# Moving the start of activation tiles by 0 to 64 bytes inside their slots, in a kernel of attention and two MoE layers

## The chip, the cores and the metric

The kernel runs on one core of a Trainium2 chip. The metric is the device time of one execution in microseconds. Before the change the median of three runs is 848.98 us (847.02 to 849.09).

## The reference

```python
# attention, per batch and head: softmax of q over the head dimension, of k over the sequence
q_s = exp(q - max(q, -1)); q_s /= sum(q_s, -1) + 1e-9
k_s = exp(k - max(k, 2));  k_s /= sum(k_s, 2) + 1e-9
kv = einsum('bhsd,bhse->bhde', k_s, v)
x = einsum('bhsd,bhde->bhse', q_s, kv)        # 4 batches, 8 heads, 576 rows, 64 columns
x = x.transpose(0, 2, 1, 3).reshape(2304, 512)
# first MoE: weights 512x2048 and 2048x512
h = x @ w_in
g = where(h >= 1, h, where(h <= -1, 0, (h + 1)**2 / 4))
x = g @ w_out
# second MoE, the same sizes
h = x @ w_in2
g = h * tanh(log1p(exp(h)))
out = g @ w_out2
```

Everything is float32.

## The kernel before

The 2304 tokens are worked in six blocks of 384 (`TB`, line 23). The first MoE and the second are done one after the other; attention for later blocks is fed in between the matmuls of earlier ones.

**Split operands.** From block 1 of the first MoE on, a float32 operand is kept as two tiles of type float32r, a high part (ScalarE copies and rounds the value) and a low part (VectorE or GpSimd subtracts the high part from the value). A product is then three matmuls: weights high by activation high, weights low by activation high, weights high by activation low (`three`, lines 510 to 513). Block 0 of the first MoE uses plain float32 matmuls instead (line 529), and so does the second layer there for its first 12 of 16 slices (line 590).

**First MoE, from block 1.** `gemm1` (line 523) makes one 128-column slice of the hidden layer in 12 matmuls of 128x384; the weights are the stationary operand, and the tiles `xh` and `xl` (made by `x_tiles`, line 262) are the moving one. The slice passes through ScalarE and VectorE, `split_high` (line 542) allocates a tile `ghl`, whose first half is the high and whose second half the low part, and three slices later (`LAG`, line 25) `gemm2` (line 582) reads it in 12 more matmuls (line 601), again as the moving operand.

**Second MoE.** It is worked in seven products instead of eight per 2x2 group of blocks (the sums that this needs are made beforehand). `unit` (line 710) makes the hidden layer: each of seven products is 6 matmuls of 128x384 with weights stationary and the activation tiles `xc` moving (allocated in `x_high`, line 703). The results are stored to DRAM and read back as `gq`, and `g_split` (line 766) splits each into two tiles `gc`. `product` (line 787) computes the output: 21 products of 72 matmuls of 128x256. Here the roles are turned round: 128-column pieces of `gc` are the stationary operand, loaded by a weight load (PEld), and the weight tiles `w2p` and `w2q` are the moving one (line 799).

**Where the tiles lie.** There are two large pools in SBUF. Weights and some activations are in pool `wp` (`big`): 36 slots of 4,096 bytes per partition. Everything else of this section is in pool `ap` (`small`, lines 119 and 120): 22 slots. A slot is as large as the largest tile of its tag. That is `v_t`, 96x2x6x65 float32 elements, 3,120 bytes a partition, which the layout rounds up to 3,136 bytes. An activation tile, 2x384 elements, takes the first 3,072 bytes of its slot. As 3,136 is 24.5 times 128, neighbouring slots begin at two places that alternate in a stretch of 128 bytes: odd slots 32 bytes and even slots 96 bytes into it. In a stretch of 256 bytes slots 0, 1, 2, 3 begin at 224, 32, 96 and 160, and then again. All weight tiles of pool `wp` begin 224 bytes into such a stretch, and so do all the pieces of them that a matmul reads, since these are 512 or 1,024 bytes apart.

**Order of the work.** The first block runs from a list of steps written out by hand (`STARTUP`). For the rest of the first MoE's blocks 1 to 4 the order on ScalarE and SyncE is the program's, that on the other engines a scheduler's (`REGIONS`, line 28); from block 5 on the order on all engines is the program's. Which slot a tile gets follows from the order in which slots come free.

Of the kernel before, what the change touches and what calls it, by code (L numbers as in the profile page):

```python
# [11 lines left out]
F32R = mybir.dt.float32r  # L12
# [7 lines left out]
P = 128  # L20
R = 96
J = 6
TB = 384
# [36 lines left out]
)  # L60
ROUND = 768.0


@with_exitstack
def tile_attention_two_moes(
# [17 lines left out]
    NP = H // 2  # L83
# [7 lines left out]
    ap = ctx.enter_context(tc.tile_pool(name="ap", bufs=22))  # L91
# [19 lines left out]
    def f(ap):  # L111
        return ap.bitcast(F32)
# [5 lines left out]

    def small(shape, dtype, name):
        return ap.tile(shape, dtype, tag="s", name=name)  # L120

    def bank(name):

        if ready:
            return a_p.tile([P, 512], F32, tag="a", name=name)
        return acc_p.tile([P, 512], F32, tag="acc", name=name)
# [16 lines left out]
    def w_stages(ph, c, m):  # L143
# [17 lines left out]
        def rounded():  # L161
            sg = f(st["t"])[:, :, 1]
            nc.scalar.activation(out=sg, in_=sg, func=AF.Copy, bias=ROUND)

# [37 lines left out]
        def sums():  # L202
            r = quarters[m, u].rearrange("p r c x -> p (r c) x")
            t = st["s"] = [small([P, 2, 2 * P], F32, "ws") for _ in range(2)]
            if m:
                t2, t3, t1, _ = (t[i // 2][:, i % 2] for i in range(4))
                add(nc.vector, t1, r[:, 1], r[:, 0])
                add(nc.gpsimd, t3, r[:, 3], r[:, 1])
                add(nc.vector, t2, r[:, 3], t1)
            else:  # L210
                s1, s2, s3, _ = (t[i // 2][:, i % 2] for i in range(4))
                add(nc.vector, s1, r[:, 2], r[:, 3], False)
                add(nc.gpsimd, s3, r[:, 0], r[:, 2])
                add(nc.vector, s2, s1, r[:, 0])
# [45 lines left out]
    xh, xl = {}, {}  # L260

    def x_tiles(ph, n):
        if n == 0:
            xh[ph, n] = [small([P, 2, TB], F32, "x0") for _ in range(NP // 2)]
            return
        xh[ph, n] = [small([P, 2, TB], F32R, "xh") for _ in range(NP // 2)]
        xl[ph, n] = [small([P, 2, TB], F32R, "xl") for _ in range(NP // 2)]

    def head_rows(a, b, c, j0, nj):
        return a[b, 2 * c:2 * c + 2].rearrange("h (p j) d -> p h j d", j=J)[:, :, j0:j0 + nj, :]  # L270
# [126 lines left out]
    def q_task(b, c, nc_, j0, nj, n, o):  # L397
# [86 lines left out]
        def x_high():  # L484
            ps = st["ps"] = st["x"][:, :nc_ * w].rearrange("p (c t) -> p c t", c=nc_)
            if (1, n) not in xh:
                x_tiles(1, n)
            st["at"] = (c // 2, (slice(None), slice(c % 2, c % 2 + nc_), slice(o, o + w)))
            i, at = st["at"]
            nc.scalar.activation(out=xh[1, n][i][at], in_=ps, func=AF.Copy)  # L490
# [5 lines left out]
        def x_split():  # L496
            x_high()
            x_low()

        if n < 2:  # L500
            return dict(
                L=load, max=row_max, sub=below, exp=exp, sum=row_sum, mul=over_sum, T=transposed, cp=copied,
                x=product, hi=x_high, lo=x_low,
            )
# [35 lines left out]
        return s[:2] == (1, 0) and s[2] < WHOLE  # L540

    def split_high(s):
        t = small([P, 2, TB], F32R, "ghl")
        gh[s], gl[s] = t[:, 0, :], t[:, 1, :]
        nc.scalar.activation(out=gh[s], in_=temps[s], func=AF.Copy)  # L545

# [3 lines left out]
    def split_g(s):  # L550
        if s[1]:
            split_high(s)
            split_low(s, eltwise(s))
# [88 lines left out]
    def high_part(hi, x):  # L642
        nc.scalar.activation(out=hi, in_=x, func=AF.Copy)  # L643

    def low_part(eng, lo, x, hi):
        eng.tensor_tensor(out=lo, in0=x, in1=f(hi), op=ALU.subtract)  # L646
# [29 lines left out]
    xq, xc = {}, {}  # L676
# [24 lines left out]
        nc.sync.dma_start(out=t, in_=src)  # L701

    def x_high(g, k, get):
        xc[g, k] = [get([P, 2, TB], F32R, "xc") for _ in range(2)]
        high_part(xc[g, k][0], xq[g, k])

    def x_low(g, k):
# [49 lines left out]
    gq, gc, sums = {}, {}, {}  # L757
# [7 lines left out]

    def g_split(at, i):
        if at < len(products):
            gc[at, i] = hi, lo = [small([P, 2, TB], F32R, "gc") for _ in range(2)]
            x = gq.pop((at, i))
            high_part(hi, x)  # L770
            low_part(nc.vector, lo, x, hi)
# [15 lines left out]
    def product(at, steps):  # L787
# [46 lines left out]
        for i in pairs:  # L834
            for which in range(2):
                for j in range(CH):
                    mm(i, j, which)
            for job in steps.pop((at, i), []):
                job()
            g_split(at + 1, i)  # L840
            g_load(at + 2, i)
# [75 lines left out]
    def startup():  # L917
        nc.vector.memset(half, 0.5)
        nc.vector.memset(unround, -ROUND)
        nc.scalar.activation(out=table, in_=half, func=AF.Exp)  # L920
# [15 lines left out]
        for c in range(NF):  # L936
            s = (1, 0, c)
            tasks[f"act{c}"] = dict(a=partial(act_scaled, s), c=partial(act_squared, s), g=partial(act_least, s), h=partial(split_high, s), l=partial(split_low, s, nc.vector))
# [77 lines left out]
    def x_operand(table, at, g, k, fetch, keep, apart):  # L1016
        put(table, at - (apart == 1), x_fetch, g, k, fetch)
        put(table, at + apart, x_high, g, k, keep)
        put(table, at + apart + 1, x_low, g, k)
# [16 lines left out]
    for g in groups[1:]:  # L1036
        for x, k_ in enumerate(ORDER):
            keep = (big if x < 3 else small) if g == 1 else big if 3 <= x < 6 else small
            at = g * per_group + (3 * x - 24 if x < 3 else 2 * x - 18)
            x_operand(places, at, g, k_, small if x in (3, 5) else big, keep, 6)  # L1040
    for u in units:
        at = groups[-1] * per_group + per_unit + u * 11 // 2
# [10 lines left out]
    for i in pairs:  # L1053
        put(places, end - 16 + i, g_load, 0, i)
        put(places, end - 8 + i, g_load, 1, i)
        put(places, end - 8 + i, g_split, 0, i)
# [3 lines left out]
    at = NF  # L1060
    for engines, upto in REGIONS:
# [3 lines left out]
        at = upto  # L1065
    with region(None):
        slot(len(slots) + LAG)
        for g in groups:
            for u in units:
                at = (g * len(units) + u) * per_unit  # L1070
# [40 lines left out]
```

## Time and profile before

| | |
|---|---|
| median of three runs | 848.98 us (847.02 to 849.09) |
| span of the profiled execution | 846.4 us |
| TensorE matmuls (PE), busy | 834.9 us, 99% of the span, 5218 instructions |
| weight loads (PEld), busy | 796.9 us, 94% |
| VectorE (DVE), busy | 582.9 us, 69% |
| ScalarE (ACT), busy | 485.9 us, 57% |
| GpSimd (POOL), busy | 350.6 us, 41% |
| 16 DMA engines, share of the span in hardware queue 1 | 63.4% |

The page gives the span of the profiled execution, from its first to its last instruction, and no other time of it; the median of the runs is 2.6 us above this span. Matmuls are pipelined, so the duration of one (some 340 ns for 384 columns) is longer than the distance from its start to the next one's start. A row of the chain that merges matmuls, such as "2.08 PE acc L601 x12", gives the time from the first one's start to the start of what follows, so 2.08 divided by 12 is the distance from start to start; a row of the timeline that merges x matmuls ends with the whole duration of the last one.

### The profile page before, as it was taken

To read this page: it belongs to the slowest core of one execution; us is meant where nothing else is said; L and a number is where in the kernel's file an instruction comes from. 1 tells how busy PE (TensorE), PEld (TensorE's weight loads), DVE (VectorE), ACT (ScalarE), POOL (GpSimd) and SP (SyncE) were. 2 spreads that over 40 slices of the span, in tenths; PEclk is the share of its full clock that TensorE was granted. 3 is DMA by queue.
4 is the path that set the end of the run, shared out by engine and by line. 5 is a ranking of instruction groups with operands and counts; after the bars stand their busy time and mean duration, and the time that the engine had idled before them with its cause. 6 is when DMAs were issued, how large, how long until landed. Compare 5 with 4: busy or idle time off the path is not lost.

```text
span 846.4 us, 14671 instructions
## 1 busy us (share of the span) xinstructions
PE 834.9 (99%) x5218; PEld 796.9 (94%) x5218; DVE 582.9 (69%) x967; ACT 485.9 (57%) x837; POOL 350.6 (41%) x325
## 2 busy tenths in 40 slices
PE   8899999999999999999999999999999999999998
PEld 8556689999999999999999999999999999999998
DVE  6999989787767676655448447765777859475553
ACT  3888687766766776676558444332444565453621
POOL 3101336424655564533455236586666566000000
PEclk9999999999999999999999999999999999999999
DMA  9999102245947462544597067877787897867933
GB/s 241 311 307 215 38 1 81 70 99 145 257 128 212 141 191 96 177 139 159 188 323 261 19 217 250 282 273 276 289 278 254 322 365 250 258 236 219 328 91 101
DMA packets 139993, 171.24 MB, mean 202 GB/s; under 512 B 57360, under 2 KB 109584, under 8 KB 139920
## 3 DMA queue, kind: packets, MB, share of 16 engines
q1 hardware_dynamic: 139680, 170.10, 63.4%
q8 instruction: 41, 0.67, 0.3%
q14 instruction: 32, 0.26, 0.1%
q10 hardware_dynamic: 240, 0.20, 0.1%
HBM read 108.40 MB, written 61.87 MB: 201 GB/s over the span
## 4 chain that ended last, share of the span: by engine, by line
PE 90%; DMA 3%; DVE 3%; SPq 2%; ACT 1%; issue 1%; POOL 0%; DVEq 0%; ACTq 0%; POOLq 0%
PE acc L601 21%; PE o L799 19%; PE m L512 7%; PE m L511 7%; PE m L513 7%; PE h L511 7%; PE h L513 7%; PE h L512 7%; PE h L529 3%; PE acc L590 2%; PE xps L482 2%; DMA gq<-gd 1%; PE kv L366 1%; DMA q_t<-in_q_dram 1%; PE qT L467 1%; SPq L308 1%
## 5 line engine op out<-in xcount | busy, mean ns | idle before, releaser
L601 PE MATMUL acc<-ghl,parts 128*128 128x384 f32 x1008 | 191.7, 339 | 0.0
L601 PEld LDWEIGHTS acc<-ghl,parts 128*128 128x128 f32 x1008 | 176.2, 188 | 0.8
L799 PE MATMUL o<-w2p,gc 128*128 128x256 f32 x1296 | 152.3, 280 | 0.6 <-POOL w2p L646 0.6
L799 PEld LDWEIGHTS o<-w2p,gc 128*128 128x128 f32 x1296 | 151.9, 189 | 0.8 <-POOL w2p L646 0.8
L643 ACT ACTIVATE gc<-gq 128x768 fp32r<-128x768 f32 x84 | 70.6, 846 | 76.5 <-DMA gq<-gd 53.4
L646 DVE TENSOR_TENSOR gc<-gq,gc 128x768 fp32r<-128x768 f32 x84 | 90.3, 1107 | 32.1 <-ACT gc L643 30.6
L511 PE MATMUL h<-xh,parts 128*128 128x384 f32 x320 | 112.0, 350 | 0.0
L567 DVE SCALAR_TENSOR_TENSOR rg<-h,rg 128x384 f32<-128x384 f32 x96 | 53.0, 552 | 81.9 <-ACT rg L562 79.8
L513 PE MATMUL h<-xh,parts 128*128 128x384 f32 x320 | 107.8, 337 | 0.0
L512 PE MATMUL h<-xl,parts 128*128 128x384 f32 x320 | 107.5, 336 | 0.0
L558 ACT ACTIVATE rg<-h,half 128x384 f32<-128x384 f32 x96 | 55.4, 577 | 82.8 <-PE h L513 73.8
L548 POOL TENSOR_TENSOR ghl<-rg,ghl 128x384 fp32r<-128x384 f32 x63 | 69.7, 1107 | 78.0 <-ACT ghl L545 74.9
L512 PE MATMUL m<-xc,w2p 128*128 128x384 f32 x288 | 96.9, 336 | 0.0
L511 PE MATMUL m<-xc,w2p 128*128 128x384 f32 x288 | 96.6, 335 | 0.0
L513 PE MATMUL m<-xc,w2p 128*128 128x384 f32 x288 | 96.6, 335 | 0.0
L736 ACT ACTIVATE high<-high 128x768 f32<-128x768 f32 x24 | 20.3, 847 | 96.9 <-DVE high L247 42.4
L512 PEld LDWEIGHTS h<-xl,parts 128*128 128x128 f32 x320 | 60.2, 188 | 1.5
L511 PEld LDWEIGHTS h<-xh,parts 128*128 128x128 f32 x320 | 60.1, 188 | 1.5
L513 PEld LDWEIGHTS h<-xh,parts 128*128 128x128 f32 x320 | 60.1, 188 | 0.0
L156 DVE SCALAR_TENSOR_TENSOR wraw<-wraw 128x512 uint32<-128x512 uint32 x64 | 57.2, 893 | 2.0
L247 POOL TENSOR_TENSOR s<-high 128x384 f32<-128x384 f32 x24 | 26.6, 1107 | 74.8 <-ACT high L736 71.7
L545 ACT ACTIVATE ghl<-rg 128x384 fp32r<-128x384 f32 x84 | 43.5, 518 | 19.3 <-DVE rg L567 17.6
(110 smaller groups left out, 1559.8 us busy)
## 6 DMA issues: line engine op xcount, KB each, us to landing
gq<-gd SPq DMA_DIRECT2D x84, 384.0 KB, 6.8
gd<-s SPq DMA_DIRECT2D x48, 384.0 KB, 3.3
wraw<-in_moe_w_in_dram SPq DMA_DIRECT2D x32, 512.0 KB, 5.9
wraw<-in_moe_w_out_dram SPq DMA_DIRECT2D x32, 512.0 KB, 4.7
gd<-low SPq DMA_DIRECT2D x24, 384.0 KB, 3.6
wk<-ws SPq DMA_DIRECT2D x32, 256.0 KB, 4.4
w<-wk SPq DMA_DIRECT2D x16, 384.0 KB, 4.3
v_t<-in_v_dram SPq DMA_DIRECT2D x32, 144.0 KB, 5.1
```

The costliest lines, as they stand in the source:

```text
L156: nc.vector.scalar_tensor_tensor(out=t[:, :, 0], in0=t[:, :, 1], scalar=3, in1=t[:, :, 0], op0=ALU.logical_shift_left, op1=ALU.bitwise_xor,)
L511: nc.tensor.matmul(ps, ah, bh, start=start, stop=False)
L512: nc.tensor.matmul(ps, ah, bl, start=False, stop=False)
L513: nc.tensor.matmul(ps, al, bh, start=False, stop=stop)
L545: nc.scalar.activation(out=gh[s], in_=temps[s], func=AF.Copy)
L548: eng.tensor_tensor(out=gl[s], in0=temps.pop(s), in1=f(gh[s]), op=ALU.subtract)
L558: nc.scalar.activation(out=t[:, 0, :], in_=hs[s][:, :TB], func=AF.Relu, scale=0.5, bias=half)
L567: nc.vector.scalar_tensor_tensor(out=g, in0=hs[s][:, :TB], scalar=1.0, in1=r, op0=ALU.max, op1=ALU.min)
L601: nc.tensor.matmul(acc[key][x][:, :TB], *pairs[at], start=first and at == 0, stop=last and at == 2)
L643: nc.scalar.activation(out=hi, in_=x, func=AF.Copy)
L646: eng.tensor_tensor(out=lo, in0=x, in1=f(hi), op=ALU.subtract)
L799: nc.tensor.matmul(ps[j][:, :QUARTER], a[:, c, js], b, start=i == c == which == 0 and b is wh, stop=i == pairs[-1] and c == which == 1,)
```

## The change

A tuple of 13 offsets (in elements of 4 bytes) is added, and a helper that allocates a flat tile of 784 elements and returns a view of 768 of them that begins 0, 4, 8, 12, 16, 6, 2, 14, 10, 1, 8, 4 or 12 elements into it. The offsets are taken in turn over all tiles that the helper makes. `xh`, `xl`, `ghl`, `gc` and those `xc` that lie in pool `ap` come from it; an `xc` in pool `wp`, the plain float32 tiles of block 0 and every other tile stay as they are. The new tile has 3,136 bytes a partition.

```diff
+SHIFTS = (0, 4, 8, 12, 16, 6, 2, 14, 10, 1, 8, 4, 12)
...
+    placed = []
+
+    def shifted(name):
+
+        at = SHIFTS[len(placed) % len(SHIFTS)]
+        placed.append(at)
+        t = ap.tile([P, 2 * TB + 16], F32R, tag="s", name=name)
+        return t[:, at:at + 2 * TB].rearrange("p (c t) -> p c t", c=2)
...
-        xh[ph, n] = [small([P, 2, TB], F32R, "xh") for _ in range(NP // 2)]
-        xl[ph, n] = [small([P, 2, TB], F32R, "xl") for _ in range(NP // 2)]
+        xh[ph, n] = [shifted("xh") for _ in range(NP // 2)]
+        xl[ph, n] = [shifted("xl") for _ in range(NP // 2)]
...
-        t = small([P, 2, TB], F32R, "ghl")
+        t = shifted("ghl")
...
-        xc[g, k] = [get([P, 2, TB], F32R, "xc") for _ in range(2)]
+        xc[g, k] = [shifted("xc") if get is small else get([P, 2, TB], F32R, "xc") for _ in range(2)]
...
-            gc[at, i] = hi, lo = [small([P, 2, TB], F32R, "gc") for _ in range(2)]
+            gc[at, i] = hi, lo = [shifted("gc") for _ in range(2)]
```

## Rows read from the trace of the kernel before

**Rows 1.** The page: span, busy time of TensorE, granted clock in 40 slices.
```profile
span 846.4 us, 14671 instructions
...
PE 834.9 (99%) x5218; PEld 796.9 (94%) x5218; DVE 582.9 (69%) x967; ACT 485.9 (57%) x837; POOL 350.6 (41%) x325
...
PEclk9999999999999999999999999999999999999999
```

**Rows 2.** The chain of work that ended last: shares of the span by engine.
```profile
PE 90%; DMA 3%; DVE 3%; SPq 2%; ACT 1%; issue 1%; POOL 0%; DVEq 0%; ACTq 0%; POOLq 0%
```

**Rows 3.** Waits of TensorE: the four longest; us in total, times, longest.
```profile
PE qT L467 <- POOL q_e L455: 3.0, 2, 1.7
PE h L529 <- DVE rg L567: 2.6, 3, 1.5
PE warm L946 <- POOL ident masks.py:199: 1.4, 1, 1.4
PE o L799 <- POOL w2p L646: 0.6, 1, 0.6
```

**Rows 4.** Groups of matmuls by line and form; count, then busy us, mean ns.
```profile
L601 PE MATMUL acc<-ghl,parts 128*128 128x384 f32 x1008 | 191.7, 339 | 0.0
L799 PE MATMUL o<-w2p,gc 128*128 128x256 f32 x1296 | 152.3, 280 | 0.6 <-POOL w2p L646 0.6
L511 PE MATMUL h<-xh,parts 128*128 128x384 f32 x320 | 112.0, 350 | 0.0
...
L511 PE MATMUL m<-xc,w2p 128*128 128x384 f32 x288 | 96.6, 335 | 0.0
...
L799 PE MATMUL o<-w2q,gc 128*128 128x256 f32 x216 | 25.7, 280 | 0.0
...
L511 PE MATMUL m<-xc,w2q 128*128 128x384 f32 x48 | 16.1, 334 | 0.0
```

**Rows 5.** The chain, 413 to 482 us: start us, us, what; one `ghl` tile each.
```profile
456.20 2.08 PE acc L601 x12
...
460.39 2.12 PE acc L601 x12
...
464.61 2.12 PE acc L601 x12
...
468.86 2.08 PE acc L601 x12
```

**Rows 6.** Timeline of PE, 786.3 to 790.2 us (odd slots) and 712.45 to 718.7 (even).
```profile
786.12 4.25 PE L799 MATMUL o<-w2q,gc 128*128 128x256 f32 x36
...
712.18 6.74 PE L799 MATMUL o<-w2p,gc 128*128 128x256 f32 x55
```

**Rows 7.** The chain, whole span: product stage, plain float32 matmuls, attention's matmuls.
```profile
52.29 2.58 PE h L529 x8
...
192.82 2.68 PE kv L366 x24
...
698.01 144.96 PE o L799 x1239
```

**Rows 8.** Groups of instructions that write the moved tiles, by form; busy us, mean ns.
```profile
L545 ACT ACTIVATE ghl<-rg 128x384 fp32r<-128x384 f32 x84 | 43.5, 518 | 19.3 <-DVE rg L567 17.6 <-PE acc L601 0.9
...
L548 POOL TENSOR_TENSOR ghl<-rg,ghl 128x384 fp32r<-128x384 f32 x63 | 69.7, 1107 | 78.0 <-ACT ghl L545 74.9 <-DMA v_t<-in_v_dram 2.1 <-POOL ghl L548 0.6
...
L643 ACT ACTIVATE gc<-gq 128x768 fp32r<-128x768 f32 x84 | 70.6, 846 | 76.5 <-DMA gq<-gd 53.4 <-PE o L799 18.9 <-DVE gc L646 2.5
...
L646 DVE TENSOR_TENSOR gc<-gq,gc 128x768 fp32r<-128x768 f32 x84 | 90.3, 1107 | 32.1 <-ACT gc L643 30.6 <-DMA gq<-gd 0.9
```

**Rows 9.** Two stretches: us, then busy us (count) of PE, PEld, DVE, ACT, POOL; clock, DMA, GB/s.
```profile
400.00:460.00 60.00, 60.00 (x344) 60.00 (x343) 32.03 (x40) 36.08 (x69) 33.73 (x26) 1.00 0.78 278
680.00:840.00 160.00, 159.45 (x1366) 159.24 (x1365) 99.40 (x137) 74.30 (x98) 29.54 (x16) 1.00 0.72 237
```

## Prediction

> **What bounds the kernel now.** I read the page first: TensorE is busy for 834.9 of 846.4 us, at the full granted clock (2.4 GHz) in all 40 slices [rows 1]. The chain says the same, 90% of it is PE [rows 2], and TensorE's waits for other engines come to about 8 us, nearly all in the first block [rows 3]. So from the end of the first block on the time is the number of matmuls times their distance from start to start, and only a change of that distance, or a new wait of TensorE, can show.
>
> Next the distances. In the first MoE 12 matmuls of 384 columns take 2.08 or 2.12 us from start to start, 173.3 or 176.7 ns each [rows 5]. In the product stage 1239 matmuls of 256 columns take 144.96 us, 117.0 ns each [rows 7]. A plain float32 matmul of 384 columns takes 2.58/8 = 322.5 ns [rows 7], or 0.84 ns a column; float32r takes half of that a column, so 173 to 177 ns is some 12 to 15 ns more than 161.2. This surplus is where a place in SBUF could count, since nothing else differs between the matmuls of one form.
>
> That it counts is in the trace. The four groups of [rows 5] have one form and differ in the tile read. By the program's layout the two of 2.08 us read `ghl` in slot 17 (32 bytes into a stretch of 256), those of 2.12 us in slots 18 and 7 (96 and 160). In the product stage the matmuls of the first of [rows 6] load their weights from odd slots: (4.25 - 0.28)/35 = 113.4 ns, with 0.28 for the last one's duration [rows 4]. Those of the second load, but for the first two, from even slots: (6.74 - 0.28)/54 = 119.6 ns. So a shift of 64 bytes is worth up to 3.4 ns a matmul of 384 columns and 6.2 of 256 columns. What a shift of 4 to 56 bytes is worth no row shows, since every start of these tiles is now 32 bytes into a stretch of 64.
>
> **The change part by part.** *Memory and order.* The new tile of 784 elements has 3,136 bytes, which the slot already has because of `v_t`. No slot grows, no other tile moves, the number of slots is the same. No instruction, DMA or wait is added or moved: 0 us.
>
> *Writing the tiles.* ScalarE, VectorE and GpSimd now write, and the low part's engine reads, at shifted places. Today the writes take 0.52 to 1.11 us each [rows 8]; no row shows them shifted. The cover: in 60 us of the first MoE these three engines are busy 36.1, 32.0 and 33.7 us, and in 160 us of the product stage 74.3, 99.4 and 29.5 us [rows 9]. Even 1.5 times as long they would fit on their engines (VectorE 149 of 160 us). A `ghl` is read three slices after it is begun, about 3 x 24 x 175 ns = 12.6 us. The `gc` of a product are made during the one before, 72 x 117 ns = 8.4 us, in which VectorE needs 4 x 1.11. Were the cover gone, 84 `ghl` late by one such write of 1.1 us each would cost 92 us; nothing in the rows leads there. I take 0.
>
> *Reading by TensorE.* Moving tiles that move: `xh` and `xl` of five blocks (960 matmuls), `ghl` (1008) and 15 of 21 pairs of `xc` (720 of 1008; the other six lie in the pool of weights), together 2688 matmuls. Stationary: all 1512 of the product stage [rows 4]. The mean offset is 388/13 = 29.8 bytes, nearly half of 64. If the distance changes evenly between known places, an odd slot in the product stage goes 0.47 of the way from 113.4 to 119.6 (2.9 ns longer) and an even slot 0.47 of the way back. Slots of both kinds are used about equally (the mean 117.0 lies near the middle of the two, 116.5), so the sum is near 0. For 384 columns the four places, in the order 224, 32, 96, 160, are fast, fast, slow, slow; moved 0.47 of the way to the next one the second loses what the fourth gains: again 0.
>
> The bounds. All at the fast level: the 384 columns gain from a mean of about 174.9 to 173.3, 1.6 x 2688 = 4.3 us, the product stage 3.6 x 1512 = 5.4 us, together 9.7 us. All at the slow level: 1.8 x 2688 + 2.6 x 1512 = 8.8 us more. Between these ends I take 0, by the even change between known places: a span of 846.4 us. The median of the runs shown is 2.6 us above that span, so the forecast is 849.0 us, no change; a measurement tells 0.3% of it, 2.5 us, from none.
>
> A rule that says the sum is exactly 0 is in the Trainium skill, "TensorE: Matmul & The Clock Gate", section "Step-by-step: what each phase is for": the weight load has a read port of its own, so loading the next weights takes nothing from the running matmul. By it alone no place of a tile could matter and the time would stay at 849.0. The trace disagrees in part: 113.4 against 119.6 ns with only the slot changed [rows 6].
>
> **The rivals.** *Pieces cut at both ends (slower).* Offsets of 6, 2, 14, 10 and 1 elements are no multiple of four. If TensorE reads pieces of four elements, such a read touches one more of them in each matmul or weight load, in all four kinds of loop. The nearest row is attention's `kv`, whose moving operand has rows of 65 elements and so begins off such pieces too: 2.68/24 = 111.7 ns against 130 x 0.84 = 109.2 by its columns, 2.5 ns more [rows 7]. Five of 13 offsets: (2688 + 1512) x 5/13 x 2.5 = 4.0 us, that is 853.0; with the slow level besides at most 861.8. It decides once the extra piece costs over 1.6 ns (2.5 us over 1615 such matmuls). For it: float32r takes its columns twice as fast as plain float32, so it has less room to hide a piece than `kv`. Against: the 2.5 ns of `kv` may as well be the weight load's. The Trainium skill, "Advanced Engine Details and Errata", section "SBUF Cachelines", gives SBUF lines of 16 bytes and a penalty for each access that goes to another line, which would make this rival real at about this price; no run here shows it for float32r.
>
> *Out of step (faster).* Now the moving and the stationary read begin at the same place of a stretch of 64 bytes, in every matmul. If the surplus comes from both being in one place at one time, 11 of the 13 offsets (all but 0 and 16 elements) break that up. All at the fast level gives 849.0 - 9.7 = 839.3; if the whole surplus of 12 ns fell at 11/13 of the 384-column matmuls it would be 27 us and more, about 820. For it: the surplus is there with float32r and not with plain float32. Against: 64 bytes change it without changing that common place, so the step within 64 bytes may count for little.
>
> *It doesn't do what it says.* Were the views laid out with no offset, everything would stay, 849.0; it shares the forecast's time.
>
> **How the numbers follow.** No measurable change 0.42 (846.5 to 851.5, with the inert case), slower 0.30 (852 to 862), faster 0.28 (839 to 846, a small part below). The size of the effects known from 64 bytes, up to 9 us either way, keeps the middle well below a half; the even spread of slots gives no sign. From the outside I leave out 0.09 below 842 (nearly all at the fast level or better) and 0.09 above 857 (pieces and slow level together). Range 842 to 857; the likeliest case's own range is 846.5 to 851.5.
>
> **What would show it.** If the steps are right: counts and rows of the writes unchanged within 2%, no new wait of TensorE, groups of 12 matmuls between 2.06 and 2.14 us with more different values than now, the product stage near 117 ns, and matmuls of one slot differing by their offset. Distances of over 178 or 121 ns at the five odd offsets alone would show the cut pieces; a fall below 172 and 113 ns at most offsets the reads out of step. Writes longer by a half, or a wait of TensorE for `ghl` or `gc`, would make the prediction wrong in its cover.

## The result and the profile after

The changed kernel takes 853.69 us (851.68 to 855.21, 4 runs) against 849.04 (847.02 to 850.07, 4 runs): a ratio of 1.0051, 95% interval 1.0027 to 1.0076. It is slower, by 2.3 to 6.5 us. The span of its profiled execution is 851.2 us, 4.8 more than before. Line numbers are 10 higher here, and 10 to 13 higher in the runs below.

The page: the span, busy time of the engines, the granted clock in 40 slices.

```profile
span 851.2 us, 14671 instructions
...
PE 839.7 (99%) x5218; PEld 801.7 (94%) x5218; DVE 582.2 (68%) x967; ACT 486.3 (57%) x837; POOL 346.5 (41%) x325
...
PEclk9999999999999999999999999999999999999999
```

The same instructions, the same clock, and TensorE busy for 4.8 us more: that is the whole difference [rows 1]. TensorE's own waits show no new one [rows 3] (that of `mT` was 0.4 us before):

```profile
PE qT L477 <- POOL q_e L465: 2.7, 2, 1.7
PE h L539 <- DVE rg L577: 2.6, 3, 1.5
PE warm L956 <- POOL ident masks.py:199: 1.4, 1, 1.4
PE mT L334 <- DVE km L329: 0.8, 1, 0.8
PE o L809 <- POOL w2p L656: 0.4, 1, 0.4
```

So the matmuls stand further apart. The chain of the changed kernel, first 413 to 486 us (`ghl` groups of 12 matmuls of 384 columns), then the product stage and a group of plain float32 matmuls; start us, us, what:

```profile
416.26 2.14 PE acc L611 x12
...
433.13 2.08 PE acc L611 x12
...
449.94 2.12 PE acc L611 x12
...
466.76 2.08 PE acc L611 x12
...
479.35 2.14 PE acc L611 x12
...
701.16 146.60 PE o L809 x1239
...
52.43 2.58 PE h L539 x8
```

The product stage needs 146.60 us for its 1239 matmuls, 118.3 ns each, against 117.0 [rows 7], and groups of 2.14 us appear, above every one of [rows 5]. Plain float32 matmuls, whose tiles don't move, stay at 2.58 us.

The program's order of instructions and the slot of every tile are the same in both kernels, so matmuls can be compared one by one. The table gives the mean distance from start to start in ns, worked out from the starts of consecutive matmuls of one stage (distances under 220 ns, to leave waits out). The stages are named by the tile that their matmuls write: acc is `gemm2` and h is `gemm1` of the first MoE from block 1 on, m is `unit` of the second. The runs below are in it too.

| kernel | acc (L601) | h | m | product stage | median us | ratio to before, 95% interval |
|---|---|---|---|---|---|---|
| before | 174.43 | 174.25 | 174.15 | 116.95 | 849.04 | |
| changed | 175.87 | 175.25 | 175.05 | 118.13 | 853.69 | 1.0051 (1.0027 to 1.0076) |
| e1, moving tiles alone | 175.87 | 175.25 | 175.05 | 116.93 | 850.66 | 1.0027 (1.0016 to 1.0038) |
| e2, `gc` alone | 174.42 | 174.25 | 174.15 | 118.15 | 849.36 | 1.0011 (1.0000 to 1.0022) |
| e3, multiples of 16 bytes | 174.78 | 175.15 | 174.70 | 118.09 | 850.92 | 1.0026 (1.0015 to 1.0037) |
| e4, placed by slot | 174.05 | 174.29 | 174.43 | 113.50 | 844.87 | 0.9945 (0.9931 to 0.9959) |
| e5, all 4 bytes | 177.54 | 177.99 | 176.71 | 118.25 | 859.69 | 1.0134 (1.0108 to 1.0160) |
| e7, all 32 bytes | 174.76 | 175.03 | 175.00 | 118.34 | 852.35 | 1.0054 (1.0036 to 1.0073) |
| e8, opposite of e4 | 175.09 | 175.68 | 174.84 | 119.18 | 853.92 | 1.0064 (1.0043 to 1.0084) |
| e9, e4 with both pools moved | 174.06 | 174.29 | 174.43 | 113.51 | 844.24 | 0.9945 (0.9929 to 0.9962) |
| e10, `gc` placed alone | 174.42 | 174.25 | 174.15 | 113.61 | 843.80 | 0.9943 (0.9928 to 0.9958) |
| e11, more moving tiles placed | 173.87 | 174.19 | 174.48 | 113.92 | 843.68 | 0.9943 (0.9928 to 0.9957) |
| e12, odd slots near the good place | 174.45 | 174.25 | 174.15 | 115.89 | 848.06 | 0.9986 (0.9975 to 0.9997) |

The sums of all distances of a stage grow by 1.4 us in acc, 0.7 in h, 0.9 in m and 1.6 in the product stage (1.8 in the distances of the table, less 0.2 of a shorter wait): 4.6 of the 4.8 us. By the offset of the moving tile, acc grows by 2.9 ns a matmul at the offsets that are no multiple of 16 bytes (4, 8, 24, 40 and 56 bytes) and by 0.4 ns at the others. In the product stage it is different: every offset of the weights loaded grows, by 0.6 to 1.7 ns, and that of 0 bytes by 1.4.

### The profile page after: what moved, and what is told of

It is laid out like the page before. It is cut to its first block, busy times and chain, and to the rows that moved or that the text cites. A ratio compares the mean times of both kernels' runs of the same rounds, so it can differ in the third digit from the quotient of the medians.

```text
span 851.2 us, 14671 instructions
## 1 busy us (share of the span) xinstructions
PE 839.7 (99%) x5218; PEld 801.7 (94%) x5218; DVE 582.2 (68%) x967; ACT 486.3 (57%) x837; POOL 346.5 (41%) x325
## 4 chain that ended last, share of the span: by engine, by line
PE 90%; DVE 4%; DMA 2%; SPq 2%; POOL 1%; issue 1%; ACT 0%; DVEq 0%; ACTq 0%; POOLq 0%
PE acc L611 21%; PE o L809 19%; PE m L523 7%; PE m L521 7%; PE m L522 7%; PE h L521 7%; PE h L522 7%; PE h L523 7%; PE h L539 3%; PE acc L600 2%; PE xps L492 2%; DMA gq<-gd 2%; PE kv L376 1%; PE qT L477 1%; SPq L318 1%; DMA q_t<-in_q_dram 1%
## 5 line engine op out<-in xcount | busy, mean ns | idle before, releaser
L558 POOL TENSOR_TENSOR ghl<-rg,ghl 128x384 fp32r<-128x384 f32 x63 | 65.4, 1038 | 79.9 <-ACT ghl L555 76.8
L166 DVE SCALAR_TENSOR_TENSOR wraw<-wraw 128x512 uint32<-128x512 uint32 x64 | 53.9, 843 | 2.0
L521 PEld LDWEIGHTS m<-xc,w2p 128*128 128x128 f32 x288 | 54.3, 188 | 0.0
```

The lines of the kernel that those rows point to most:

```text
L166: nc.vector.scalar_tensor_tensor(out=t[:, :, 0], in0=t[:, :, 1], scalar=3, in1=t[:, :, 0], op0=ALU.logical_shift_left, op1=ALU.bitwise_xor,)
L521: nc.tensor.matmul(ps, ah, bh, start=start, stop=False)
L558: eng.tensor_tensor(out=gl[s], in0=temps.pop(s), in1=f(gh[s]), op=ALU.subtract)
```

## The experiments

Two theories stood at first. **Cut pieces**: a read that begins off a multiple of 16 bytes touches one more piece of four elements. **Mixed places**: what costs is that tiles that follow each other no longer begin alike. Later runs add a third, the **place** of one read relative to the other.

**Which of the two operands.** One run shifts the moving tiles alone, the other the stationary ones alone.

```diff
# e1
-            gc[at, i] = hi, lo = [shifted("gc") for _ in range(2)]
+            gc[at, i] = hi, lo = [small([P, 2, TB], F32R, "gc") for _ in range(2)]
# e2
-        at = SHIFTS[len(placed) % len(SHIFTS)]
+        at = SHIFTS[len(placed) % len(SHIFTS)] if name == "gc" else 0
```

> Only the tiles that TensorE reads as moving operand (xh, xl, ghl, xc) are shifted, in the cycle of 13; gc, the stationary operand of the product stage, begins at its slot again. Cut pieces: the matmuls of 384 columns keep the 3.0 us by which their distances grew in the changed kernel (1.4 us in line acc, 0.7 in h, 0.9 in m), the product stage falls back to 117.0 ns a matmul: 852 us. Mixed places (what costs is that neighbouring tiles begin at different places): the same split, 852 us; this run only sizes the two parts. If the parts need each other (the changed kernel's 4.7 us is not the sum), it comes out at 849 or at 853.7.

> Only gc is shifted, in the same cycle; the moving tiles begin at their slots. The product stage should be as in the changed kernel, 118.1 ns a matmul against 117.0, 1.6 us in all: 850.6 us, and lines h, acc and m as before (174 ns). Cut pieces: those weight loads that begin off a multiple of 16 bytes carry it. Mixed places: it is spread over all offsets, with those of 0 bytes among them.

The table shows a clean split: e1 has the changed kernel's distances in acc, h and m to 0.01 ns and the old one's in the product stage, e2 the reverse. The product stage in the chain, first e1:

```profile
700.13 144.97 PE o L809 x1239
```

then e2:

```profile
699.06 146.63 PE o L809 x1239
```

In time e1 costs 0.27% and e2 0.11% (0.00 to 0.22). In e2 the growth was spread over all offsets again (0.7 to 1.7 ns, 1.3 at 0 bytes), which speaks against cut pieces as its cause.

**Without offsets that cut a piece.**

```diff
-SHIFTS = (0, 4, 8, 12, 16, 6, 2, 14, 10, 1, 8, 4, 12)
+SHIFTS = (0, 4, 8, 12, 16, 4, 0, 12, 8, 0, 8, 4, 12)
```

> All five kinds of tile are shifted, but each offset that is no multiple of 4 elements (16 bytes) is lowered to the next one that is. Cut pieces: the matmuls of 384 columns lose nearly all of their 3.0 us, only the product stage's 1.6 us can stay: 849 to 850.6 us. Mixed places: as many different places meet as before, so nothing comes back: 853 to 854 us.

850.92 us, with 1.6 us of growth left in acc, h and m together (0.35, 0.66 and 0.55) and 1.3 in the product stage (1.7 in its distances, less a shorter wait). So about half of the moving tiles' 3.0 us went with the cut pieces, and the product stage hardly changed. Neither theory alone fits.

**All offsets alike.**

```diff
# e5
-SHIFTS = (0, 4, 8, 12, 16, 6, 2, 14, 10, 1, 8, 4, 12)
+SHIFTS = (1,)
# e7
+SHIFTS = (8,)
```

> Every shifted tile begins 1 element (4 bytes) into its slot: all reads are off a multiple of 16 bytes, and all in the same way. Cut pieces: the 384-column matmuls grow as those of this offset did in the changed kernel (2.9 ns in acc, 4.7 in h, 3.4 in m, about 10 us in all) and the weight loads of the product stage by 1 to 2.5 ns (2 to 4 us): 860 to 863 us. Mixed places: nothing is mixed, so the distances go back to 174.3 and 117.0 ns: 849 us.

> Every shifted tile begins 8 elements (32 bytes) into its slot, so all begin at a multiple of 64 bytes, while the weights stay 32 bytes off one. Cut pieces: none is cut, 849 us within 2. Mixed places: 849 us. Out of step (the third way of the prediction): both reads now differ by 32 bytes within 64 everywhere, the surplus over the columns shrinks, the 384-column matmuls fall to 172 ns or less and the product stage to 113.4 or less: under 840 us.

With 4 bytes everywhere nothing is mixed, and the 384-column matmuls grow by 2.6 to 3.7 ns on average (in m 288 of 1008 read tiles that stay). With 32 bytes everywhere they grow by 0.3 to 0.9 ns. In the chain of e5, from 413 us on, 2.14 to 2.16 us is the common level and the shortest of 17 groups has 2.09:

```profile
415.19 2.16 PE acc L611 x12
...
457.94 2.16 PE acc L611 x12
462.24 2.09 PE acc L611 x12
466.45 2.14 PE acc L611 x12
```

So e3 and e5 show that a moving read pays for a start off a multiple of 16 bytes, also where every tile is shifted alike; that it is the extra piece which costs was not seen by itself. The product stage has 118.25 ns with cut weight loads (e5) and 118.34 without (e7), though these differ in place as well: a cut costs a weight load nothing that shows, and being uniform doesn't bring 117.0 back either. "Out of step" fell with e7: 32 bytes between the two reads makes them slower, not faster.

**The place.** e4 picks the offset by the slot that a tile gets, e8 does the opposite, e9 is e4 with both pools moved.

```diff
# e4, gc: 64 bytes in even slots, 0 in odd; moving tiles: 0, 0, 32, 64 bytes
+PLACE = {"gc": (16, 0, 16, 0)}
-        at = SHIFTS[len(placed) % len(SHIFTS)]
+        at = PLACE.get(name, (0, 0, 8, 16))[SLOTS[len(placed)] % 4]
# e8
+PLACE = {"gc": (0, 16, 0, 16)}
+        at = PLACE.get(name, (0, 16, 0, 0))[SLOTS[len(placed)] % 4]
# e9, on top of e4
+    const.tile([P, 16], F32, name="spare")
     half = const.tile([P, 1], F32, name="half")
```

> The offset is chosen by the slot that the tile gets: 0 or 64 bytes for gc, so that every gc begins 32 bytes into a stretch of 128 (odd slots' place before); 0, 0, 32 or 64 bytes for the moving tiles in slots 0, 1, 2, 3 of four, so that they begin at 224, 32, 128 and 224 of 256. If the place within 128 or 256 bytes sets the distance: product stage from 117.0 to 113.4 to 115 ns (3 to 5.4 us), the 384-column matmuls from 174.3 to about 173.5 (2 us): 842 to 845 us, under both kernels. If what made odd slots fast before was not their place but what lay around them: 848 to 850 us.

> The opposite of the placed kernel: gc gets 64 bytes in odd slots and 0 in even ones, so that all begin at even slots' place (96 into 128), and moving tiles in slots 1 of four get 64 bytes, so that they begin at 96, 160 or 224 of 256. If the place sets the distance: product stage 119 to 119.7 ns a matmul (3.0 to 4.1 us more), acc up by about 1 ns: 852.5 to 855 us. If offsets of 0 and 64 bytes by themselves are good: under 849 us.

> The placed kernel with a spare tile of 64 bytes ahead of both pools: weights and activations move by 64 bytes together. If the distance hangs on the place of one read relative to the other, all stays as in the placed kernel: product stage 113.5 ns, 844.9 us. If it hangs on each one's own place within 128 bytes, gc is now at the slow place: product stage 119 to 120 ns, 853 to 855 us.

e4 takes 844.87 us, under both kernels. Its product stage in the chain:

```profile
696.61 140.70 PE o L810 x1239
```

That is 113.6 ns each, 4.3 us less than in [rows 7], and 113.5 for the whole stage; the tiles of even slots, moved by 64 bytes, went from 118.9 to 113.5 ns. e8 goes the other way, to 119.18 ns; in its chain the whole stage is one row, without a wait:

```profile
666.72 180.20 PE o L810 x1512
```

In e9 `gc` begins 96 bytes into a stretch of 128, the place that was slow before, and so do the weights that stream past it:

```profile
696.93 140.72 PE o L811 x1239
```

The same as e4, and acc, h and m are the same too, to 0.01 ns. So it is not a tile's own place that counts but its place relative to the other operand's: the weight load is fast when it begins 64 bytes, modulo 128, from where the moving operand begins.

The traces show two things more. First, the good place pays in full only in long runs of it. In the kernel before, odd slots have 115.2 ns on the mean and even ones 118.9; the first two distances after a change to an odd slot average 117.7 ns, the 3rd to the 20th 115.0 to 115.8, and from the 21st on it is 113.4 to 113.7. In the changed kernel a tile at the good place mostly stands alone among others, and has 117.6 ns. So mixing has a part in the product stage: an odd slot's tile that got 0 bytes and stayed where it was went from 115.4 to 117.8 ns.

Second, moving reads have places as well, in a stretch of 256 bytes. In acc before, the tiles that begin 64, 0, 192 and 128 bytes past the weights have 173.0, 174.2, 175.2 and 176.2 ns. e8 takes those at 64 to 128, and the tiles at 128 have 176.1 ns; e4 takes those at 192 to 0, and the tiles at 0 have 173.9. In e3, where no piece is cut, acc lies between 173.3 ns (64 bytes past) and 176.8 (240).

**How much of it is `gc`, and is there more.**

```diff
# e10
+        at = PLACE.get(name, (0, 0, 0, 0))[SLOTS[len(placed)] % 4]
# e11
+        at = PLACE.get(name, (16, 0, 8, 16))[SLOTS[len(placed)] % 4]
```

> Only gc is moved, 64 bytes in even slots and 0 in odd ones, as in the placed kernel; the moving tiles begin at their slots. If the product stage's place is what pays: 113.5 ns a matmul there, 4.6 to 5.2 us less than before, and lines acc, h and m as before (174.4, 174.3, 174.2 ns): 844 to 845 us, within 0.5 us of the placed kernel. If the placed moving tiles had a part in it: 847 us or more.

> gc as in the placed kernel; the moving tiles of slots 0 and 1 of four begin 64 bytes past the weights' place in a stretch of 256 (offsets 64 and 0 bytes), those of slots 2 and 3 as in the placed kernel. If 64 bytes past the other operand is the good place for moving reads too, acc falls from 174.0 to 173.6 ns, h and m by 0.3 to 1 ns: 843 to 844.5 us. If not: as the placed kernel, 844.5, or up to 1 us over it.

`gc` alone gives 843.80 us, all of the gain:

```profile
697.54 140.85 PE o L810 x1239
```

In e11 every one of the 16 `ghl` groups of the stretch from 413 us on takes 2.08 us, but h stays, m grows by 0.3 ns, and the time is the same, 843.68 us.

**How wide the good place is.** `gc` gets 64 bytes in even slots; in odd slots 0, 4, 8, 16 or 32 bytes, in turn by product.

```diff
+NEAR = (0, 1, 2, 4, 8)
+        at = 0 if name != "gc" else 16 if SLOTS[n] % 2 == 0 else NEAR[(n - FIRST) // 8 % 5]
```

> Only gc is moved: 64 bytes in even slots; in odd slots 0, 4, 8, 16 or 32 bytes, in turn by product, so that in one product of five all begin at the good place and in the others the odd slots lie 4, 8, 16 or 32 bytes past it. If the good place is narrow: products with 4 bytes or more already have 116 to 118 ns a matmul against 113.5, and the whole comes out near 848 us. If the distance changes evenly between known places, as the prediction had it: 113.6, 113.9, 114.2 and 115 ns, and the whole near 845.5 us.

848.06 us, as "narrow" had it. The timeline of TensorE over five products that follow each other, with 0, 4, 8, 16 and 32 bytes in the odd slots; start us, us, then the count at the end:

```profile
790.77 8.32 PE L812 MATMUL o<-w2p,gc 128*128 128x256 f32 x72
...
798.71 8.86 PE L812 MATMUL o<-w2p,gc 128*128 128x256 f32 x74
...
807.17 8.79 PE L812 MATMUL o<-w2p,gc 128*128 128x256 f32 x74
...
815.57 8.71 PE L812 MATMUL o<-w2p,gc 128*128 128x256 f32 x73
...
823.99 8.73 PE L812 MATMUL o<-w2p,gc 128*128 128x256 f32 x74
```

With 0.28 us off for the last one's duration these are 113.2, 117.5, 116.6, 117.1 and 115.8 ns a matmul, though only part of the tiles lie in odd slots. Worked out from the starts, tiles at the place itself have 113.8 to 115.5 ns in all five kinds of product, and those 4, 8, 16 and 32 bytes past it 118.1, 118.6, 118.2 and 117.5. Four bytes are enough to lose nearly all of it (e8, with no tile at the place, has 119.2).

## Why the prediction was right and wrong

*The range and the frame held.* 853.69 us lies in 842 to 857, which reached from a gain to a loss; it does not lie in the likeliest case's own 846.5 to 851.5, but in the case "slower", which had a chance of 0.30. That the time is the number of matmuls times their distance, that no instruction or wait is added and no other tile moves, is what the after profile shows.

*The forecast of no change did not hold, and the step that failed is "If the distance changes evenly between known places".* In the product stage the good place is a narrow one. The odd slots of the old kernel lay in it. Of the 13 offsets only 0 leaves an odd slot there, and only 64 bytes brings an even slot to it. Before, 797 of the stage's 1509 distances were at the place; after, 132 are. The sum had 2.9 ns lost in odd slots and as much gained back in even ones. Odd slots lost 2.9 ns (115.2 to 118.0), but even ones gained only 0.7 (118.9 to 118.2): 117.0 went to 118.1 ns, 1.6 us, where the sum had 0. That the 2.9 came out is luck: it was 0.47 of 6.2 ns, read from two stretches of 35 and 53 matmuls in a row at one place, and is three quarters of the 3.8 ns by which the two kinds of slot differ over the whole stage.

*For the 384 columns the even change failed too.* They grew by 3.0 us. Split by the offset of the tile that each matmul reads, 1.9 of them are at the five offsets off 16 bytes, a cost that the sum had at nothing, and 1.1 at the rest, where the place changes without a cut. The mean that the bounds started from was high as well: 174.9 ns, where the three stages have 174.2 to 174.4.

*The rival "pieces cut at both ends" had the time right (853.0) and half of the reason.* Its price was 2.5 ns at 4200 x 5/13 matmuls, 4.0 us. For moving reads e5 shows the cost, at 2.6 to 3.7 ns. For weight loads none shows: 118.25 against 118.34 ns with and without the cut, and in e12 118.1 and 118.6 (cut) against 118.2 and 117.5. What it overcounted there, the lost place gave back, which it didn't name; that the total came so near is luck. The Trainium skill, "Advanced Engine Details and Errata", section "SBUF Cachelines", with its lines of 16 bytes, agrees with e5 and e3 for moving reads, but has no price; for weight loads no run shows its penalty.

*The rival "out of step" was wrong* for both kinds of matmul: e7, with the two reads 32 bytes apart, has acc, h and m 0.3 to 0.9 ns and the product stage 1.4 ns longer, and is 0.54% slower. The surplus of 12 ns that it counted on hangs on float32r taking just half of plain float32 a column, 161.2 ns for 384; no run shows that, and the shortest distance of acc, h and m in the kernel before and the changed one is 168 ns.

*The rule on a read port of its own* ("TensorE: Matmul & The Clock Gate" in the Trainium skill, section "Step-by-step: what each phase is for") does not hold here as far as the prediction drew it out, that no place could matter: e10 moves nothing but where the next weights are read, and the product stage goes from 116.95 to 113.61 ns.

*The bounds were of use.* "All at the fast level" had 5.4 us for the product stage, reckoned at 113.4 ns. e4 reaches 113.5 ns, 5.2 us in the distances and 4.6 with a wait for `w2p` that is longer by 0.5; e10 gains 5.2 us on the medians. For the 384 columns acc comes near the fast level (173.87 ns in e11, 2.08 us in the stretch looked at), h and m do not by these offsets.

*The cover held, its detail did not.* The prediction said that the rows of the writes would stay within 2%. ScalarE's do (518 and 846 ns). VectorE's part of `ghl` went from 767 to 915 ns on the mean, but not by the place: 19 of its 21 writes stay within 35 ns, and two go from 0.54 to 2.57 and 1.64 us, both while a GpSimd instruction runs that did not overlap them before. In e4, e9 and e11, which move `ghl` too, the mean is 767. GpSimd's part went from 1107 to 1038 [rows 8], and this goes with the offset: 867 ns at the median with 4 bytes everywhere (e5), 1017 with 32 (e7), 1022 before. No wait of TensorE came of either. The rows, VectorE's before, then both of the changed kernel:

```profile
L548 DVE TENSOR_TENSOR ghl<-rg,ghl 128x384 fp32r<-128x384 f32 x21 | 16.1, 767 | 3.1 <-ACT ghl L545 3.0
...
L558 DVE TENSOR_TENSOR ghl<-rg,ghl 128x384 fp32r<-128x384 f32 x21 | 19.2, 915 | 3.1 <-ACT ghl L555 3.0
...
L558 POOL TENSOR_TENSOR ghl<-rg,ghl 128x384 fp32r<-128x384 f32 x63 | 65.4, 1038 | 79.9 <-ACT ghl L555 76.8 <-DMA v_t<-in_v_dram 2.1 <-issue 1.0
```

Two things stay open: why 64 bytes, modulo 128, between the two reads is good, and only in a long run of such loads in full (no run looked into the memory itself), and how the 1.6 us by which acc, h and m still grow in e3, where no piece is cut, divide between the place of each moving tile and its neighbours'.

## What to carry to other kernels

When TensorE is busy throughout, compare the start-to-start distances of matmuls of one form before looking for anything else: two levels that go with a tile's slot mean that addresses matter. Here float32r reads wanted moving tiles at multiples of 16 bytes, and weight loads 64 bytes, modulo 128, from the moving operand, many of them in a row. Since a pool's slot size sets where tiles begin, choose it (or an offset per slot) for that; a mixture of offsets leaves the good place nearly everywhere.

## What the runs showed that was not expected

- The distances repeat almost exactly: stages that an edit leaves alone have the same mean to 0.03 ns in different runs (acc 174.43, 174.42, 174.45; m 174.15 each time), so a stage's distance tells apart what the medians, with 2 us between runs, cannot.
- The good place of the product stage is narrower than 4 bytes on the side tried in e12: 114.2 ns at it, 118.1 ns 4 bytes past it. It goes with the two operands' distance and not with either's address (e4 and e9: 113.50 and 113.51 ns).
- A moving tile that begins 4 bytes past a multiple of 16 costs each 384-column matmul some 3 ns, 1.5 to 2% of its distance; a weight load pays nothing that shows.
- GpSimd's subtraction of 128x384 elements is shorter, not longer, with its tile off a multiple of 16 bytes: 867 ns at the median in e5 against 1022 before, and 866 to 892 at the five such offsets of the changed kernel against 1014 to 1027 at its others.
